# S4 convolution and gated linear attention: three small vectors loaded as rows and turned on TensorE, one table ahead of two copies

## The chip, the core and the metric

The kernel runs on one core of a Trainium2 chip. The metric is the device time of one execution in microseconds (us). A core has five engines that run their own instruction streams in order and wait for each other by semaphores: TensorE (PE; its weight loads are shown apart as PEld), VectorE (DVE), ScalarE (ACT), GpSimd (POOL) and SyncE (SP), which here issues the DMA transfers between HBM and the on-chip memory SBUF. TensorE writes its results to PSUM, from where VectorE or ScalarE copy them out.

## The reference

Two branches work on the same input x = u of [1, 2048, 512] (bfloat16) and are mixed by a gate:

```python
g = sigmoid((x * gate_w).sum(-1, keepdims=True))
a = _A_ref(x, A_re, A_im, B_re, B_im, C_re, C_im, log_dt, Dskip)   # S4: long convolution + skip
b = _B_ref(x, wqkv, w_phi, wo)                                     # linear attention, 32 heads of 16
return g * a + (1 - g) * b
# _A_ref: dt = exp(log_dt); K[d, l] = Re sum_n C exp(dt A l) dt B;  y = irfft(rfft(u) * rfft(K)) + u * Dskip
# _B_ref: phi = [softmax(k w_phi), softmax(-k w_phi)];  o = phi_q (phi_k' v) / (phi_q sum phi_k);  o @ wo
```

Three vectors of 512 numbers matter here: log_dt (the step size of each channel), gate_w (the weights of the gate) and Dskip (the weights of the skip connection).

## The kernel before

The whole kernel is one list of nodes (class `Plan`, L71). A node is a small piece of work on one engine, with what it reads and writes, and, if it needs one, a PSUM tile. The order in which the nodes are emitted, and with it the order on every engine, is written out in a table, `ORDER` (two characters for each node, numbered as they were added). `SIDES` says for each copy out of PSUM (`evict`) whether VectorE or ScalarE makes it; `RINGS` says for each TensorE node that may choose from which ring its PSUM tile comes. There are two such rings in the part that matters, `ps` (digit 0) and `p0` (digit 1), with two buffers each; a third tile in a ring waits until the first one has been read out. Adding a node renumbers those behind it, so the strings differ in many places where the order does not.

What runs in the first 30 us:

- SP issues the loads: sixteen of u in rows (`UD`, L1531, four for each quarter; a node `ud0` to `ud3` is a quarter), the weights `wqk` (L1541, 1 MB) and `WW` (L1544), the six S4 matrices `Are` to `Cim` (L214), and the small vectors. `ldc` (log_dt, L1526), `gw` (gate_w, L1537) and `Dcol_b` (Dskip, L1538) are loaded by column: a tile of 128 partitions with four elements of two bytes in each, number g of partition p being element 128 g + p of the vector. `ld` (L1527) is log_dt once more, broadcast to all partitions.
- VectorE and ScalarE build tables of phases (`tgv`, `tgsv`, `TB`, `TJ`, `TI`) from iota patterns; GpSimd makes the iotas and `Wphi`. `selE` (L456) is one of the tables of VectorE, which takes two small masks (`m`, `b`) and no load.
- TensorE transposes u, eight blocks at a time, into an `xps` tile (L502; eight groups, T8 = 0 to 7, group T8 needs quarter T8 // 2 of u), which is copied to `xT` by VectorE (L149) or ScalarE (L147). T8 = 0 and T8 = 4 come first, before wqk is there, and VectorE copies both. Of the six late groups VectorE copies T8 = 6, ScalarE the rest.
- The columns of wqk are transposed (`wtp`, L528) to `wT`, multiplied by `Wphi` (`wps`, L544), and copied to `WW` and `Wqp`. Of the first two wtp tiles VectorE copies the second one first, and the other after a table instruction.
- The S4 matrices are transposed in pairs (`psri`, L368): pB = (Bre, Bim), pC = (Cre, Cim), pA = (Are, Aim). VectorE multiplies them with the steps (`p_t`, L381) to `ppx`, `pt`, `pmag`, `ppy`. A psri tile is let go when the second product that reads it alone has run: for pB the second of two, for pA the second of two.
- Of the discretised A, pt and ppy are cast and subtracted (L343, L344); SP stores the result to DRAM (`pz`, L348).
- VectorE copies u to `UDp`, and TensorE begins the spectrum of u with it (`psA`, L589), copied to `XAu` by VectorE and ScalarE. Behind this the main part starts: the keys of the attention (`pk`, `Ek`, `Zk`, `vp`), then queries, tables and convolution.

In RINGS, the digits of the eight xps groups are 00000111 and those of pB, pC, pA are 101: T8 = 5, 6 and 7, pB and pA take their tiles from p0, the others from ps.

Of the kernel before, what the change touches and what calls it, by code (L numbers as in the profile page):

```python
# [10 lines left out]
ACT = mybir.ActivationFunctionType  # L11
# [185 lines left out]
def prepare(P, nc, g, evict, psum):  # L197
# [39 lines left out]
    V("ident", lambda: nc.vector.tensor_scalar(out=g.ident[:], in0=g.c128[:], scalar1=g.icol["p"], scalar2=None, op0=ALU.is_equal), r="ic1", w="ic")  # L237

# [255 lines left out]
    E("at3", at3, r="ic wsm mask", w="atm")  # L494
    xt = []
    for T8 in range(8):
        box = Bag()

        def tx(T8=T8, box=box):
            box.ps = psum([128, 4, 4, 4, 32], "xps", BF16)  # L500
            for t in range(8):
                nc.tensor.transpose(out=box.ps[:, t // 4, :, t % 4, :], in_=g.UD[:, 8 * T8 + t, :], identity=g.ident[:])  # L502

        def xe(T8=T8, box=box):
# [1160 lines left out]
```

## Time and profile before

| | |
|---|---|
| median of 3 runs | 254.35 us (252.84 to 256.95) |
| the profiled execution | 252.56 us |
| its span (first to last instruction) | 250.7 us |
| VectorE busy | 233.6 us, 93% |
| ScalarE busy | 222.0 us, 89% |
| TensorE matmuls busy | 201.7 us, 80% |
| DMA | 35.65 MB in 62762 packets, 42112 of them under 512 B |

The profile is of one execution. A group of instructions is printed as start and duration in us, engine, line of the kernel, operation, out<-in with sizes, and how many instructions it joins (x3); the durations of one instruction in its group overlap a little with the next one's, so the time from one start to the next is the pace. In brackets stands the idle time of the engine ahead of the group and what ended it. In the list of idle times a row has the engine, its line, what it waited for, and then the total, how often, and the longest. PE, PEld, DVE, ACT, POOL are the engines, SPq is SP's queue of DMA issues.

### The profile page before, as it was taken

The page shows a single profiled execution, that of the slowest core. Times are in us where ns is not written, and L with a number is a line of the kernel's source. Part 1 is how long each engine was busy: PE and PEld are TensorE (multiplying, and loading weights), DVE is VectorE, ACT ScalarE, POOL GpSimd, SP SyncE. Part 2 cuts the span into 40 slices and gives each one's busy share as a digit, 9 for nine tenths or more (in the row PEclk, how much of TensorE's full clock was granted, in tenths as well). Part 3 has the DMA queues.
Part 4 walks back from the last instruction along what each step waited for, and adds up shares of the span by engine and source line. Part 5 has one row for each costly group of instructions (what it writes and reads, how often), then busy time and mean ns, then how long its engine had stood idle before and what let it go on. Part 6 is the DMA issues. An engine that isn't in the chain of part 4 may idle for free.

```text
span 250.7 us, 9903 instructions
## 1 busy us (share of the span) xinstructions
PE 201.7 (80%) x4411; PEld 141.6 (56%) x4436; DVE 233.6 (93%) x322; ACT 222.0 (89%) x306; POOL 6.3 (2%) x15
## 2 busy tenths in 40 slices
PE   1478899999965468798878778899999789998970
PEld 1377555456743334255556646775667566877550
DVE  6899999989899997999999999999999999999690
ACT  6799899999999989999999999999999999965340
POOL 5400000000000000000000000000000000000000
PEclk9999999999997759999979999999999999999995
DMA  6799200137290487500528138803797878998775
GB/s 167 162 211 164 77 4 3 42 94 191 53 259 0 126 245 224 169 3 4 151 63 235 30 101 222 277 11 86 189 207 191 222 213 212 239 243 151 184 184 82
DMA packets 62762, 35.65 MB, mean 142 GB/s; under 512 B 42112, under 2 KB 58624, under 8 KB 62336
## 3 DMA queue, kind: packets, MB, share of 16 engines
q1 hardware_dynamic: 62720, 35.03, 57.1%
q8 instruction: 34, 0.56, 1.0%
q14 instruction: 8, 0.07, 0.1%
HBM read 21.91 MB, written 13.11 MB: 140 GB/s over the span
## 4 chain that ended last, share of the span: by engine, by line
DVE 40%; PE 19%; ACT 16%; SPq 8%; issue 8%; DMA 7%; DVEq 0%; ACTq 0%
DVE R L1126 5%; DVE t L1302 4%; DVE A L1109 4%; DMA XUX<-XUd 3%; ACT Eq L68 3%; PE vp L755 3%; SPq L1531 3%; DVE A L1114 3%; PE pk L707 3%; DVE R L1130 3%; DVE Zk L734 2%; SPq L214 2%; DVE E L1061 2%; PE psB L614 2%; DVE Eq L912 2%
## 5 line engine op out<-in xcount | busy, mean ns | idle before, releaser
L181 PEld LDWEIGHTS <-A 128*32 128x32 bf16 x1664 | 28.4, 160 | 6.3 <-issue 3.4
L181 PE MATMUL kps<-R,A 128*32 128x64 bf16 x1664 | 30.2, 230 | 1.9 <-DVE A L1114 0.6
L68 ACT ACTIVATE cs<-args 128x1024 bf16<-128x1024 f32 x32 | 30.8, 1049 | 0.4 <-PE args L1025 0.4
L1130 DVE TENSOR_TENSOR R<-E,cs 128x2048 bf16<-128x2048 bf16 x16 | 19.5, 1220 | 0.0
L1109 DVE TENSOR_TENSOR A<-Ctab,Dtab 128x2048 bf16<-128x2048 bf16 x16 | 19.5, 1220 | 0.0
L1126 DVE TENSOR_TENSOR R<-E,cs 128x2048 bf16<-128x2048 bf16 x16 | 19.5, 1220 | 0.0
L1114 DVE TENSOR_TENSOR A<-Ctab,Dtab 128x2048 bf16<-128x2048 bf16 x16 | 19.5, 1220 | 0.0
L147 ACT CAST Zr<-psz 128x1024 bf16<-128x1024 f32 (+1 forms) x17 | 16.5, 975 | 2.7 <-issue 1.2
L147 ACT CAST XK<-psB 128x1024 bf16<-128x1024 f32 (+1 forms) x15 | 15.1, 1012 | 3.9 <-PE psB L194 2.3
L147 ACT CAST XA<-psA 128x1024 bf16<-128x1024 f32 (+1 forms) x16 | 15.6, 1008 | 3.2 <-PE psA L188 3.2
L755 PE MATMUL vp<-WW,xT 128*128 128x512 bf16 x59 | 17.5, 414 | 0.8 <-issue 0.7
L614 PE MATMUL psB<-XAu,TB 64*128 64x128 bf16 x256 | 11.8, 248 | 7.4 <-ACT xst L147 5.2
L1302 DVE TENSOR_TENSOR t<-XUX,XK 128x2048 bf16<-128x2048 bf16 x14 | 17.1, 1220 | 0.3 <-ACT XK L147 0.3
L68 ACT ACTIVATE Ek<-pk 128x512 bf16<-128x512 f32 x32 | 16.8, 603 | 0.4 <-PE pk L707 0.2
L68 ACT ACTIVATE Eq<-pq 128x512 bf16<-128x512 f32 (+1 forms) x28 | 16.8, 715 | 0.2 <-PE pq L841 0.2
L68 ACT ACTIVATE E<-args 128x1024 bf16<-128x1024 f32 x16 | 16.8, 1060 | 0.0
L1328 PE MATMUL psz<-t,TI 128*128 128x512 bf16 x49 | 14.6, 380 | 2.0 <-ACT cs L68 0.5
L841 PE MATMUL pq<-xT,Wqp 128*128 128x512 bf16 x64 | 15.7, 381 | 0.6 <-ACT Eq L68 0.6
L614 PEld LDWEIGHTS <-TB 64*128 64x128 bf16 x256 | 9.5, 109 | 11.3 <-issue 11.1
L707 PE MATMUL pk<-WW,xT 128*128 128x512 bf16 x57 | 15.5, 380 | 0.5 <-issue 0.2
L734 DVE TENSOR_REDUCE Zk<-Ek 128x64 f32<-128x1024 bf16 x12 | 14.0, 1211 | 0.0
L65 ACT ACT_TABLE_LOAD x10 | 12.8, 1283 | 0.2
(215 smaller groups left out, 492.4 us busy)
## 6 DMA issues: line engine op xcount, KB each, us to landing
XUX<-XUd SPq DMA_DIRECT2D x24, 256.0 KB, 4.1
XUd<-xst SPq DMA_DIRECT2D x8, 512.0 KB, 3.1
ax<-apd SPq DMA_DIRECT2D x16, 256.0 KB, 4.7
Zd<-Zr SPq DMA_DIRECT2D x14, 256.0 KB, 4.0
ZT<-Zd SPq DMA_DIRECT2D x12, 256.0 KB, 5.3
UD<-in_A_u_dram SPq DMA_DIRECT2D x16, 128.0 KB, 4.2
XUd<-xst SPq DMA_DIRECT2D x8, 256.0 KB, 4.0
XUX<-XUd SPq DMA_DIRECT2D x4, 512.0 KB, 6.3
```

The lines of the kernel that those rows point to most:

```text
L68: return self.nc.scalar.activation(**kw)
L147: self.nc.scalar.copy(out=o, in_=i)
L181: nc.tensor.matmul(kps[32 * dj:32 * dj + 32, g4, e, :], lhsT=A[:, ka, :, :, d].rearrange("p a b -> p (a b)"), rhs=R[:, kr, d, :], start=(i ...
L614: nc.tensor.matmul(box.ps[:, c2, sl, :], lhsT=fc.TB[rows, b0:b0 + 2].rearrange("p a b -> p (a b)"), rhs=X.t[rows, k, r0 + sl].rearrange("p ...
L707: nc.tensor.matmul(box.ps[:], lhsT=xT[:, st, kt, :], rhs=g.WW[:, kt, :], start=(kt == 0), stop=(kt == 3))
L734: nc.vector.tensor_reduce(out=K.Z[:, u].rearrange("p g h -> p (g h)"), in_=K.E[:, u].rearrange("p g (h f) -> p (g h) f", f=16), axis=mybir ...
L755: nc.tensor.matmul(box.ps[:], lhsT=xT[:, st, kt, :], rhs=g.WW[:, 4 + kt, :], start=(kt == 0), stop=(kt == 3))
L1109: nc.vector.tensor_tensor(out=c.A[:, 0:2].rearrange("p o a b c -> p (o a) b c"), in0=g.C[U // 8][:, 0:2, :, d0 % 256:d0 % 256 + 32].rearra ...
L1114: nc.vector.tensor_tensor(out=c.A[:, 2:4].rearrange("p o a b c -> p (o a) b c"), in0=g.C[U // 8][:, 1:3, :, d0 % 256:d0 % 256 + 32].rearra ...
L1126: nc.vector.tensor_tensor(out=c.R[:, :, :, 32:64], in0=t.E[:, 1].unsqueeze(1).to_broadcast([128, 2, 32, 32]), in1=t.cs[:], op=ALU.mult)
L1130: nc.vector.tensor_tensor(out=c.R[:, :, :, 0:32], in0=t.E[:, 0].unsqueeze(1).to_broadcast([128, 2, 32, 32]), in1=t.cs[:, ::-1, :, ::-1], o ...
L1302: nc.vector.tensor_tensor(out=box.t, in0=Ls[r0 // ns].X[:], in1=box.XK[:].unsqueeze(1).to_broadcast([128, 2, 1024]), op=ALU.mult)
```

## The change

The three loads by column go. In their place SP loads each vector as four rows of 128 contiguous elements: 12 rows of 256 bytes together, into the first 12 partitions of `zrow` (a tile that is not used until the gate is computed much later). TensorE turns these 12 rows with one more transposition, right behind the eight of T8 = 4 and into the same PSUM tile (its third, unused, slot). VectorE copies the 128x12 result to a tile `vecs`, of which ldc, gw and Dcol_b are now slices.

The nodes of xps and xT are added earlier in the list (the order of adding, not of running), and the strings ORDER, SIDES and RINGS are new. The rings of the xps and psri tiles are the same as before. The order differs in these places; names are those of the tiles with a running number, which counts differently in the two programs.

SP, from its first instruction: UD, then wqk and the small loads. Before:

```order
L1531 DMA UD<-in_A_u_dram 32x16x128 x4
L1541 DMA wqk<-in_B_wqkv_dram 128x4x1024
L214 DMA Are<-in_A_A_re_dram 128x4x128
L1536 DMA wc<-in_B_w_phi_dram 128x4x16
L1537 DMA gw<-in_gate_w_dram 128x4x1
L1538 DMA Dcol_b<-in_A_Dskip_dram 128x4x1
L214 DMA Aim<-in_A_A_im_dram 128x4x128
L214 DMA Bre<-in_A_B_re_dram 128x4x128
L1526 DMA ldc<-in_A_log_dt_dram 128x4x1
L1527 DMA ld<-in_A_log_dt_dram 128x512
```

And now:

```order
L1541 DMA UD_105<-in_A_u_dram 32x16x128 x4
L1537 DMA zrow_69<-in_A_log_dt_dram 4x128
L1537 DMA zrow_69<-in_gate_w_dram 4x128
L1537 DMA zrow_69<-in_A_Dskip_dram 4x128
L1549 DMA wqk_113<-in_B_wqkv_dram 128x4x1024
L214 DMA Are_106<-in_A_A_re_dram 128x4x128
L1546 DMA wc_114<-in_B_w_phi_dram 128x4x16
L214 DMA Aim_107<-in_A_A_im_dram 128x4x128
L214 DMA Bre_109<-in_A_B_re_dram 128x4x128
L1533 DMA ld_112<-in_A_log_dt_dram 128x512
```

The three row loads stand ahead of wqk; the three loads by column, which stood behind it, are gone.

VectorE in the late stage, from the product of Aim with the step to the first products of pA (psri_374 before, psri_414 now; pB is psri_317 in both). Before:

```order
L341 TENSOR_TENSOR pt0_163<-Aim_108,dt2_306 128x512
L381 TENSOR_TENSOR ppx_160<-psri_317,pt2_165 128x512
L343 CAST pt1_164<-pt0_163 128x512
L344 TENSOR_TENSOR pt1_164<-pt0_163,pt1_164 128x512
L381 TENSOR_TENSOR ppx_160<-psri_317,pt2_165 128x512
L149 COPY UDp_395<-UD_106 128x16x2x32
L381 TENSOR_TENSOR pt0_163<-psri_374,pt2_165 128x512
```

And now:

```order
L364 TENSOR_TENSOR pt0_161<-Aim_107,dt2_306 128x512
L404 TENSOR_TENSOR ppx_158<-psri_317,pt2_163 128x512
L366 CAST pt1_162<-pt0_161 128x512
L149 COPY xT_68<-xps_398 128x1024
L367 TENSOR_TENSOR pt1_162<-pt0_161,pt1_162 128x512
L404 TENSOR_TENSOR ppx_158<-psri_317,pt2_163 128x512
L149 COPY UDp_426<-UD_105 128x16x2x32
L404 TENSOR_TENSOR pt0_161<-psri_414,pt2_163 128x512
```

The copy of T8 = 6 (xps_398; before it was xps_445, the last instruction ahead of the first XAu cast) now stands between the cast and the subtraction.

ScalarE in the same stage, from the second WW cast. Before:

```order
L147 CAST WW_85<-wps_273 128x1024
L147 CAST Wqp_84<-wps_336 128x1024
L147 COPY xT_68<-xps_348 128x1024
L147 COPY xT_68<-xps_363 128x1024
L147 COPY xT_68<-xps_383 128x1024
L147 CAST Wqp_84<-wps_408 128x1024
L147 COPY xT_68<-xps_422 128x1024
L147 COPY xT_68<-xps_432 128x1024
```

And now:

```order
L147 CAST WW_85<-wps_273 128x1024
L147 CAST Wqp_84<-wps_336 128x1024
L147 COPY xT_68<-xps_348 128x1024
L147 COPY xT_68<-xps_359 128x1024
L147 COPY xT_68<-xps_369 128x1024
L147 COPY xT_68<-xps_379 128x1024
L147 COPY xT_68<-xps_388 128x1024
L147 CAST Wqp_84<-wps_438 128x1024
```

The five copies now follow each other, and the second Wqp cast stands behind them. xps_388, the fifth, is T8 = 7.

On TensorE the transpositions of Are and Aim, those of Cre and Cim, and the second wps of Wqp, which stood between the late xps groups, now stand behind all six of them, in that order; T8 = 6 (xps_398) is the last of the six. Early on VectorE, `selE` stood behind the two copies of T8 = 0 and T8 = 4 and now stands ahead of them, and the copy to `vecs` stands between the two. GpSimd's order is the same.

The diff, with the strings cut to their first lines and what only renames left out:

```diff
-    ORDER = ("0H0I000K0J0M190S0L0s0t0u0U0W0X0B0C0D0T0d0e0f2x0y0z0A2L2v0g0h0i2J2K2M2y2R0102031d2w0N0_0Y0V2T100j0k0l0P1114120405060Z2U16"
...
+    ORDER = ("0K0L00120M141t1a130v0w0x0m0n0o1c1e1f0E0F0G1b0d0e0f2R0B0C0D0Y2P2Q0g0h0i0Z0V0W0X2S2V0102031x151j1g1d2X1k0j0k0l171l1o1m0405"
...
-    SIDES = ("100001110111000000000101000101010111101001011100000000000100101010000001110001001010100000000000000010000000000000000000"
+    SIDES = ("000011101111000000000101000101010111101001011100000000000100101010000001110001001010100000000000000010000000000000000000"
...
-    RINGS = ("101000001110010101100000000000000000000000100000000000000001011100100000001111101101110000100001001110011110100111101101"
+    RINGS = ("000001111010010101100000000000000000000000100000000000000001011100100000001111101101110000100001001110011110100111101101"
...
-    P.dma("ld", 0.8, 2.0, lambda: g.load_ld(), rw=("", "ldc ldb"), move=0.5, cnt=2)
+    P.dma("ld", 0.8, 2.0, lambda: g.load_ld(), rw=("", "ldb"), move=0.5)
+    P.dma("rows", 1.5, 2.0, lambda: g.load_rows(), rw=("", "rows"), move=0.1, cnt=3)
...
-    P.dma("wsm", 1.5, 2.0, lambda: g.load_small(), rw=("", "wsm"), move=0.6, cnt=3)
+    P.dma("wsm", 0.5, 2.0, lambda: g.load_small(), rw=("", "wsm"), move=0.3)
...
+        def tx(T8=T8, box=box):
+            box.ps = psum([128, 4, 4, 4, 32], "xps", BF16)
+            for t in range(8):
+                nc.tensor.transpose(out=box.ps[:, t // 4, :, t % 4, :], in_=g.UD[:, 8 * T8 + t, :], identity=g.ident[:])
+            if T8 == 4:
+                nc.tensor.transpose(out=box.ps[:, 2, 0, 0, 0:12], in_=g.rows, identity=g.ident[0:12, 0:12])
+
+        def cw(box=box):
+            nc.vector.tensor_copy(out=g.vecs[:], in_=box.ps[:, 2, 0, 0, 0:12])
...
+        a = P.add("PE", "xps", tx, take=[("ps", "p0")], rw=(f"ud{T8 // 2} ic" + (" rows" if T8 == 4 else ""), ""))
+        cv = [V("cvec", cw, w="wsv ldc", deps=[a])] if T8 == 4 else []
+        xt.append(evict("xT", xe, [a] + cv))
...
-        g.gw = aq.tile([128, 4], BF16, name="gw")
-        g.Dcol_b = aq.tile([128, 4], BF16, name="Dcol_b")
+        g.vecs = aq.tile([128, 12], BF16, name="vecs")
+        g.ldc, g.gw, g.Dcol_b = g.vecs[:, 0:4], g.vecs[:, 4:8], g.vecs[:, 8:12]
+        g.rows = g.zrow[0:12, 0, 0:64].bitcast(BF16)
...
         def load_ld():
-            with nc.allow_non_contiguous_dma(reason="small"):
-                nc.sync.dma_start(out=g.ldc[:], in_=A_log_dt.rearrange("(g p) -> p g", p=128))
             nc.sync.dma_start(out=g.ld_b[:], in_=A_log_dt.partition_broadcast(128))
+
+        def load_rows():
+            for k, v in enumerate((A_log_dt, gate_w, A_Dskip)):
+                nc.sync.dma_start(out=g.rows[4 * k:4 * k + 4], in_=v.rearrange("(g p) -> g p", p=128))
...
-                nc.sync.dma_start(out=g.gw[:], in_=gate_w.rearrange("(kt p) -> p kt", p=128))
-                nc.sync.dma_start(out=g.Dcol_b[:], in_=A_Dskip.rearrange("(kt p) -> p kt", p=128))
```

More of the change, by code (lines that the diff above doesn't have):

```diff
@@ L237, in prepare, with xe @@
     V("ident", lambda: nc.vector.tensor_scalar(out=g.ident[:], in0=g.c128[:], scalar1=g.icol["p"], scalar2=None, op0=ALU.is_equal), r="ic1", w="ic")
+    xt = []
+    for T8 in range(8):
+        box = Bag()
+        def tx(T8=T8, box=box):
[6 more added lines that the diff above has]
+            nc.vector.tensor_copy(out=g.vecs[:], in_=box.ps[:, 2, 0, 0, 0:12])
+        def xe(T8=T8, box=box):
+            i = box.ps[:, 0:2]
+            box.ps = None
+            return g.xT[:, 2 * T8:2 * T8 + 2].rearrange("p j k s -> p (j k s)"), i.rearrange("p j k c q -> p (j k c q)")
+        a = P.add("PE", "xps", tx, take=[("ps", "p0")], rw=(f"ud{T8 // 2} ic" + (" rows" if T8 == 4 else ""), ""))
+        cv = [V("cvec", cw, w="wsv ldc", deps=[a])] if T8 == 4 else []
+        xt.append(evict("xT", xe, [a] + cv))
     P.add("POOL", "iota", lambda: iota_f(nc, F.col[:], [[16, 32], [1024, 64]], 8), rw=("ic0", "col"))
@@ L327, in dtc @@
         F.dtc = g.up.tile([128, 4], F32, name="dtc")
-        act(out=F.dtc[:], in_=g.ldc[:], func=ACT.Exp)
+        act(out=F.dtc[:], in_=g.ldc, func=ACT.Exp)
     S("dtc", dtc, r="act ldc", w="dtc")
@@ L493, in at3 @@
         nc.gpsimd.memset(at.eps[:], 1e-6)
[L494 to L504, printed above, removed]
-            i = box.ps[:, 0:2]
-            box.ps = None
-            return g.xT[:, 2 * T8:2 * T8 + 2].rearrange("p j k s -> p (j k s)"), i.rearrange("p j k c q -> p (j k c q)")
-        a = P.add("PE", "xps", tx, take=[("ps", "p0")], rw=(f"ud{T8 // 2} ic", ""))
-        xt.append(evict("xT", xe, [a]))
+    E("at3", at3, r="ic wsv mask", w="atm")
     kp = fold(P, nc, g, evict, psum, 512, lambda: g.WW[:, 0:4, :], "wT1")
@@ L677, in gc @@
         nc.vector.reciprocal(out=g.gT[:], in_=G.z[:])
-    a = P.add("PE", "gps", ga, xt, take=["ps"], rw=("wsm", ""))
+    a = P.add("PE", "gps", ga, xt, take=["ps"], rw=("wsv", ""))
     b = P.add("DVE", "g_b", gb, [a], drop=["psum"])
```

45 lines of the change are left out of this document (22 added, 23 removed).

## The prediction

> **What bounds the kernel now.** I read the first part of the profile's page, then the busy time by stretches of the span, then the chain of waits and the idle times of the first 34 us, the only part in which the change moves anything. The page:
>
> ```profile
> span 250.7 us, 9903 instructions
> PE 201.7 (80%) x4411; PEld 141.6 (56%) x4436; DVE 233.6 (93%) x322; ACT 222.0 (89%) x306; POOL 6.3 (2%) x15
> ```
>
> VectorE (DVE) is busy for 93% of the span and ScalarE (ACT) for 89%. A share of the whole span hides where the slack is, so the next view gives stretches (length, then busy time of PE, PEld, DVE, ACT, POOL, the granted clock, DMA share, GB/s):
>
> ```profile
> core 0: us, PE busy (x) PEld busy (x) DVE busy (x) ACT busy (x) POOL busy (x), PEclk, DMA share, GB/s
> 20.00:28.00 8.00, 5.96 (x79) 5.04 (x79) 7.96 (x16) 6.99 (x9) 0.00 (x0) 1.00 0.79 159
> 28.00:60.00 32.00, 31.34 (x546) 17.59 (x553) 31.11 (x43) 30.78 (x59) 0.00 (x0) 1.00 0.21 58
> 100.00:150.00 50.00, 41.35 (x1056) 26.84 (x1055) 49.54 (x58) 49.82 (x74) 0.00 (x0) 0.97 0.34 97
> 150.00:200.00 50.00, 44.44 (x1134) 33.53 (x1138) 49.97 (x54) 48.71 (x58) 0.00 (x0) 1.00 0.69 173
> ```
>
> From 20 to 28 us VectorE idles 0.04 us; from 28 to 60 it idles 0.89 of 32, and later 0.46 and 0.03 of 50. So whatever the first 28 us lose or gain on VectorE goes through to the end almost one to one; there is no slack behind to swallow it. What VectorE did at the edge of that stretch, from the chain of waits (start, us, what):
>
> ```profile
> 5.88 3.09 SPq L214
> ...
> 18.16 3.86 DMA UD<-in_A_u_dram
> 22.02 0.02 issue
> 22.04 0.42 DVE UDp L149
> ```
>
> The chain walks back from the first UDp copy through a load of the input and SP's queue. But the load landed at 22.02 and VectorE, which had been busy without a pause, came to it at 22.04: a tie. Loads that land earlier buy nothing unless VectorE also comes earlier.
>
> **The late stage: the moved copy.** This is the large term. VectorE's and ScalarE's rows of that place in the trace of before:
>
> ```profile
> 20.38 0.42 DVE L343 CAST pt<-pt 128x512 bf16<-128x512 f32 x1
> 20.83 0.69 DVE L344 TENSOR_TENSOR pt<-pt,pt 128x512 bf16<-128x512 f32 x1
> 21.44 0.68 DVE L381 TENSOR_TENSOR ppx<-psri,pt 128x512 f32<-128x512 f32 x1
> 22.04 0.42 DVE L149 COPY UDp<-UD 128x1024 bf16<-128x1024 bf16 x1
> ...
> 26.96 0.68 DVE L149 COPY xT<-xps 128x1024 bf16<-128x1024 bf16 x1
> 27.56 1.22 DVE L149 CAST XAu<-psA 128x1024 bf16<-128x1024 f32 x1
> ```
>
> ```profile
> 20.58 2.85 ACT L147 COPY xT<-xps 128x1024 bf16<-128x1024 bf16 x3
> 23.66 1.01 ACT L147 CAST Wqp<-wps 128x1024 bf16<-128x1024 f32 x1 [0.22 <-PE wps L544]
> 24.57 1.94 ACT L147 COPY xT<-xps 128x1024 bf16<-128x1024 bf16 x2
> ```
>
> ```profile
> 15.73 1.91 PE L528 MATMUL wtp<-ident,wqk 128*128 128x128 bf16 x16
> 19.43 1.33 PE L502 MATMUL xps<-ident,UD 128*128 128x128 bf16 x16
> 20.73 0.38 PE L368 MATMUL psri<-ident,Are 128*128 128x128 bf16 x4
> 20.95 0.39 PE L368 MATMUL psri<-ident,Aim 128*128 128x128 bf16 x4
> 21.65 0.61 PE L502 MATMUL xps<-ident,UD 128*128 128x128 bf16 x8 [0.31 <-ACT xT L147]
> ```
>
> VectorE's only late xT copy stood at 26.96, last before the XAu cast, where its input had been ready for long. The change puts it right behind the cast at 20.38. That copy reads the xps group of T8 = 6, and this group's PSUM tile comes from ring p0, as those of T8 = 5 and 7 and of psri for pB and pA do. p0 has two buffers. One still holds psri of pB (Bre, Bim), because the second product that reads it stands behind the moved copy on VectorE. So the other passes from T8 = 7 to T8 = 6 to psri of pA. TensorE can start T8 = 6 only when T8 = 7 has been copied out, and that is the fifth xT copy of ScalarE, which now stand in one run ahead of the second Wqp cast. VectorE works in order: behind the waiting copy are queued the subtraction of 20.83, pB's second product, all four UDp copies, the products of pA and pC, and XAu. For UDp in turn TensorE's psA waits, then ScalarE's XAu and all Ek work.
>
> The size: three copies took 2.85 us and two 1.94, so one comes 0.91 after the other (difference of the rows) and the last runs about 1.03. Five from 20.58 end at 20.58 + 4 x 0.91 + 1.03 = 25.25. TensorE's eight transpositions take 0.61: 25.86; I allow 0.15 for the two hand-overs (ACT to PE, PE to DVE; no row has them apart): 26.0. VectorE is free at 20.38 + 0.42 = 20.80. It idles 5.2 us. The copy itself is the same work in another place (26.96 to 27.56, 0.60). The rest, 20.83 to 26.96, is 6.13, so XAu starts at 26.0 + 0.60 + 6.13 = 32.7 instead of 27.56: **+5.2**.
>
> The psri of pA, Are and Aim, follow the copy (0.38 and 0.39, overlapping, 0.61 together) and are hidden by the subtraction, the product and the UDp copy, which start 0.61 and 0.60 apart and end with 0.42. The psA matmuls now come straight behind their UDp copies, and the second Wqp cast comes to ScalarE behind its own wait; what stood there at leisure is now in line with VectorE. I take 0.3 for it, between 0 and the 0.8 that ScalarE idled for psA here already (row below). With it: **+5.5**.
>
> ```profile
> 27.82 1.01 ACT L147 CAST XAu<-psA 128x1024 bf16<-128x1024 f32 x1 [0.79 <-PE psA L589]
> 32.30 1.03 PE L755 MATMUL vp<-WW,xT 128*128 128x512 bf16 x4
> ```
>
> SP's store of pz also waits for that subtraction, and the WW load behind it in SP's queue goes out some 5 us later; its reader, vp at 32.30, moves by as much, so nothing is added.
>
> **The start: the row loads.** SP's rows, the idle times, and the rows between:
>
> ```profile
> 2.75 0.49 SPq L1541 DMA_DIRECT2D wqk<-in_B_wqkv_dram  x1
> ...
> 4.38 0.72 SPq L1537 DMA_DIRECT2D gw<-in_gate_w_dram  x1
> 5.15 0.69 SPq L1538 DMA_DIRECT2D Dcol_b<-in_A_Dskip_dram  x1
> ```
>
> ```profile
> DVE xT L149 <- PE xps L502: 1.7, 1, 1.7
> PE wtp L528 <- DMA wqk<-in_B_wqkv_dram: 2.0, 1, 2.0
> ```
>
> ```profile
> 8.48 1.22 DVE L456 TENSOR_TENSOR selE<-m,b 128x1024 bf16<-128x1024 bf16 x1
> 11.88 0.68 DVE L149 COPY wT<-wtp 128x1024 bf16<-128x1024 bf16 x1
> 17.31 0.17 DVE L333 TENSOR_SCALAR dt<-dtc 128x4 f32<-128x4 f32 x1
> ```
>
> ```profile
> 9.20 1.89 PE L528 MATMUL wtp<-ident,wqk 128*128 128x128 bf16 x16 [1.96 <-DMA wqk<-in_B_wqkv_dram]
> ```
>
> ```profile
> GB/s 0 15 224 203 164 340 356 350 66 18 195 72 131 211 242 205 208 213 211 203 191 215 162 148 71 243 240 0 0 0 0 0 0 0 0 0 16 8 0 0
> wqk<-in_B_wqkv_dram SPq DMA_DIRECT2D x1, 1024.0 KB, 6.4
> gw<-in_gate_w_dram SPq DMA_DIRECT2D x1, 1.0 KB, 5.9
> ```
>
> selE (1.22) fills the 1.7 us in which VectorE waited for xps; the new copy to vecs costs between 0.1 and 0.2 (the nearest row is the 128x4 dt, 0.17). The extra weight load and 12-column matmul on TensorE are at most one of the 0.12 us transpositions (1.89 / 16). VectorE would be some 1.4 us (1.7 less 0.17 and a hand-over of 0.1) earlier at its first wT copy, 10.5 instead of 11.88. But that copy needs all 16 wtp transpositions, hence wqk, and wqk is now issued behind three row loads of about 0.54 us each: at 4.38 instead of 2.75. It landed 6.4 after issue, at 9.15. Two bounds: with the same 6.4 it lands at 10.8. In the GB/s row (one number per us) the four early UD loads, issued from 0.74 on, moved first bytes in the second us, some 1.3 us after issue; wqk's three full slots, 5 to 8, came behind them. If wqk was merely queued, it now starts 1.3 behind its issue at 5.7, moves for 3.0 and lands 1.1 later, as it did: 9.8. The wT copy then starts 9.8 + 1.89 + 0.1 = 11.8 (no change) or 12.8 (+0.9). I take 10.2 to 10.3, +0.5, nearer the queued case, since TensorE's wait of 1.96 shows that wqk had only its bytes to wait for. wT starts the chain that leads to ScalarE's xT copies (wps, the wtp of wT2, WW, Wqp), so this comes on top: **+0.5**, between -0.7 (wqk unmoved) and +0.9.
>
> The element-wise loads that go cost SP 0.72 and 0.69, and the load behind them 3.09 (above). [...] In my sum it is worth 0: the loads come earlier, by up to that 3.09, and VectorE doesn't.
>
> **Sum:** 5.5 + 0.5 = +6.0. On the profiled execution, 252.56 (span 250.7 and 1.86 around it), 258.6. The median of the runs shown is 254.35 (252.84 to 256.95), with it 260.4. I put the forecast between: **259.5**. Within 2%, 5.1 us, is about what a measurement of this kernel can't tell from no change.
>
> **The rivals.**
> *The loads decide, and nothing waits (not slower).* If VectorE's moved copy finds T8 = 6 ready at 20.8, which needs a free p0 buffer some 4.5 us before ScalarE's fifth copy ends, the stage keeps its length. Then the start's 1.4 us, or at most SP's 3.09, come through: 249.5 to 251.2. For it speaks the chain, which runs through SP and the UD load; against it the tie at 22.02, and above all the order of the copies. Chance 0.10.
>
> *The wait comes, but smaller.* wqk lands early (-0.7), ScalarE starts its five copies earlier than 20.58, and idle pieces between 60 and 100 us, the least filled stretch, take some of it back:
>
> ```profile
> 60.00:100.00 40.00, 28.52 (x492) 19.23 (x494) 37.19 (x65) 37.97 (x53) 0.00 (x0) 0.83 0.52 145
> ```
>
> VectorE idles 2.8 us there, ScalarE 2.0. If 1 us is given back beside the 0.7 and the 0.5 not spent: +3.5 to +5, 256.5 to 258.5. Chance 0.18.
>
> *The wait comes and TensorE slows down.* At 15.73 us 16 transpositions took 1.91, at 21.65 8 took 0.61: nearly half the pace against full, with the change of pace inside the 16 of 19.43 (1.33). In the changed kernel TensorE idles some 1.9 us ahead of T8 = 6 and 3 to 4 us ahead of psA. If it falls back to half pace, T8 = 6 costs 0.6 more and the first psA and pk matmuls 1 to 1.5: +7 to +8, about 261 to 262. [...] No run here shows a fall back yet. Chance 0.12.
>
> *The rows land late.* The neighbour gw took 5.9 us from issue to landing; so long a time puts the last row load (issued at 3.8) at 9.7, and VectorE's vecs copy, with selE done, waits for it from about 8 on. Under 9 us the wait is hidden by that for wqk; at 9.7 TensorE's early groups and wtp come late too: +6.5 to +7.5. Chance 0.04.
>
> My forecast, +5 to +7, has what is left, 0.56. Slower by over 2%: 0.56 + 0.12 + 0.04, less 0.05 for the part of the forecast near 5.1 us: 0.67. Faster by over 2%, past anything a load is worth here: 0.03. Within 2%: 0.30. The range leaves out the first rival (0.10) and a tail above: 256.0 to 262.8.
>
> **What will show it.** Right, if VectorE idles about 5 us ahead of an xT copy on PE's xps, TensorE waits 1 to 2 us for ScalarE's xT ahead of that group, and XAu starts near 33; if wtp still waits for wqk, which lands at 9.8 or later; if SP's 3.09 us is gone and the UD loads land earlier, without use. Wrong, if that xT copy starts by 22 us, if UDp waits for its load again, or if the shift at 60 us is not the shift at the end.

## The result, and the profile after

The changed kernel takes 261.92 us (median of 6 runs, 260.24 to 265.93) against 254.72 of the kernel before (6 runs, 252.84 to 257.01): 1.0298 times as long, with a 95% interval of 1.0253 to 1.0343. That is some 7.2 to 7.6 us more. The profiled execution of this measurement was a slow one (265.93), so the rows below are those of a second measurement of the same kernel, which gave 1.0294 [1.0248, 1.0339] and whose profiled execution took 261.46.

Its page and its busy time by stretches (us; busy PE, PEld, DVE, ACT, POOL; granted clock, DMA share, GB/s):

```profile
span 259.7 us, 9932 instructions
PE 207.3 (80%) x4437; PEld 143.0 (55%) x4437; DVE 234.5 (90%) x323; ACT 222.1 (86%) x306; POOL 5.6 (2%) x15
```

```profile
20.00:24.00 4.00, 2.04 (x28) 1.58 (x26) 0.67 (x2) 4.00 (x5) 0.00 (x0) 0.97 0.74 107
24.00:28.00 4.00, 2.12 (x19) 1.87 (x18) 1.76 (x3) 1.13 (x2) 0.00 (x0) 0.50 0.01 1
28.00:34.00 6.00, 3.19 (x23) 2.62 (x22) 5.43 (x12) 1.54 (x2) 0.00 (x0) 0.50 0.42 111
```

VectorE does the same work (234.5 us against 233.6) in a longer span. From 20 to 28 us, where it was busy for 7.96 of 8, it now works 2.43. And the clock that TensorE is granted reads 0.50 from 24 to 34 us; in the profile of before it read 1.00 in all of these stretches.

VectorE, ScalarE and TensorE in the late stage of the changed kernel:

```profile
20.25 0.42 DVE L366 CAST pt<-pt 128x512 bf16<-128x512 f32 x1
26.23 0.69 DVE L149 COPY xT<-xps 128x1024 bf16<-128x1024 bf16 x1 [5.56 <-PE xps L247]
...
33.62 1.23 DVE L149 CAST XAu<-psA 128x1024 bf16<-128x1024 f32 x1 [0.57 <-PE psA L597]
...
38.17 1.23 DVE L149 CAST XAu<-psA 128x1024 bf16<-128x1024 f32 x1 [1.71 <-PE psA L597]
```

```profile
20.34 4.80 ACT L147 COPY xT<-xps 128x1024 bf16<-128x1024 bf16 x5
```

```profile
21.44 0.61 PE L247 MATMUL xps<-ident,UD 128*128 128x128 bf16 x8 [1.23 <-DMA UD<-in_A_u_dram]
22.36 0.61 PE L247 MATMUL xps<-ident,UD 128*128 128x128 bf16 x8 [0.31 <-ACT xT L147]
23.38 0.70 PE L247 MATMUL xps<-ident,UD 128*128 128x128 bf16 x8 [0.42 <-DMA UD<-in_A_u_dram]
25.18 1.01 PE L247 MATMUL xps<-ident,UD 128*128 128x128 bf16 x8 [1.10 <-ACT xT L147]
...
32.51 1.93 PE L597 MATMUL psA<-W,UDp 128*128 128x256 bf16 x8 [2.81 <-DVE UDp L149]
34.23 3.46 PE L715 MATMUL pk<-WW,xT 128*128 128x512 bf16 x8
```

And of the kernel before, the rows of psA and pk on TensorE and the second XAu on VectorE:

```profile
26.51 1.19 PE L589 MATMUL psA<-W,UDp 128*128 128x256 bf16 x8 [1.10 <-ACT xT L147]
27.54 1.89 PE L707 MATMUL pk<-WW,xT 128*128 128x512 bf16 x7
```

```profile
30.31 1.22 DVE L149 CAST XAu<-psA 128x1024 bf16<-128x1024 f32 x1
```

Read from below: VectorE's moved copy waits 5.56 us for T8 = 6 (25.18), which TensorE begins 1.10 us after it could, when ScalarE's fifth copy is done (20.34 + 4.80 = 25.14). The first XAu comes 6.06 us later than before (33.62 against 27.56), the second 7.86 (38.17 against 30.31): between the two another 1.8 us are lost, where TensorE does psA in 1.93 instead of 1.19 and eight pk in 3.46, where seven took 1.89.

Behind that nothing is gained or lost for most of the span. One of the late VectorE rows, first of before and then of the changed kernel:

```profile
180.11 1.22 DVE L1302 TENSOR_TENSOR t<-XUX,XK 128x2048 bf16<-128x2048 bf16 x1
```

```profile
188.38 1.22 DVE L1310 TENSOR_TENSOR t<-XUX,XK 128x2048 bf16<-128x2048 bf16 x1
```

That is 8.27 us behind, 150 us after the place where the time was lost. Near the end VectorE loses some more: it waits 1.20 us for psy where it waited 0.52, and 2.33 for bps where it waited 1.24, and the spans differ by 9.0 (259.7 against 250.7). What causes this was not tried. The traces show more than the 7.2 to 7.6 us of the times partly because the profiled execution of before, 252.56, lies below its median.

The start, with SP's loads, the first wT copies on VectorE and what GpSimd does beside them:

```profile
2.76 0.43 SPq L1537 DMA_DIRECT2D zrow<-in_A_log_dt_dram  x1
3.23 0.25 SPq L1537 DMA_DIRECT2D zrow<-in_gate_w_dram  x1
...
3.86 0.41 SPq L1549 DMA_DIRECT2D wqk<-in_B_wqkv_dram  x1
...
6.85 2.09 SPq L1533 DMA_DIRECT2D ld<-in_A_log_dt_dram  x1
```

```profile
9.69 0.81 DVE L290 TENSOR_SCALAR tgv<-tgc,one 128x1024 int32<-128x1024 f32 x1 [0.15 <-ACT TB L68]
11.13 0.69 DVE L149 COPY wT<-wtp 128x1024 bf16<-128x1024 bf16 x1 [0.62 <-PE wtp L536]
11.73 1.55 DVE L290 TENSOR_SCALAR tgv<-tgc,one 128x1024 int32<-128x1024 f32 x1
13.21 0.67 DVE L149 COPY wT<-wtp 128x1024 bf16<-128x1024 bf16 x1
```

```profile
9.20 1.89 PE L536 MATMUL wtp<-ident,wqk 128*128 128x128 bf16 x16 [1.20 <-DMA wqk<-in_B_wqkv_dram]
```

```profile
11.79 0.95 POOL L791 MEMSET KVbd<- 128x1024 bf16 x1
```

The second of these wT copies in the kernel before:

```profile
13.33 0.67 DVE L149 COPY wT<-wtp 128x1024 bf16<-128x1024 bf16 x1
```

wqk is issued 1.1 us later than before, and still wtp begins at 9.20, as before. VectorE reaches its first wT copy 0.75 us early, and is 0.12 early at the second (13.21 against 13.33), where the table instruction between them takes 1.55 us, 0.92 before; GpSimd clears KVbd beside it.

### The profile page after: what moved, and what is told of

Its sections match the earlier page's. It is cut to its first block, busy times and chain, and to the rows that moved or that the text cites. A ratio compares the mean times of both kernels' runs of the same rounds, so it can differ in the third digit from the quotient of the medians.

```text
span 264.1 us, 9932 instructions
## 1 busy us (share of the span) xinstructions
PE 208.5 (79%) x4437; PEld 144.5 (55%) x4437; DVE 234.8 (89%) x323; ACT 222.4 (84%) x306; POOL 5.5 (2%) x15
## 4 chain that ended last, share of the span: by engine, by line
PE 27%; ACT 25%; DVE 23%; DMA 9%; SPq 7%; issue 7%; DVEq 0%; ACTq 0%
PE pk L715 5%; ACT cs L68 5%; ACT Eq L68 4%; SPq L1541 4%; PE vp L763 3%; ACT E L68 3%; PE psB L622 2%; DMA ZT<-Zd 2%; DVE t L1310 2%; PE kps L181 2%; DMA XUd<-xst 2%; ACT XA L147 2%; PE psy L830 2%; ACT L65 2%; DVE vr L772 2%
## 5 line engine op out<-in xcount | busy, mean ns | idle before, releaser
L715 PE MATMUL pk<-WW,xT 128*128 128x512 bf16 x64 | 17.7, 412 | 0.0
L1336 PE MATMUL psz<-t,TI 128*128 128x512 bf16 x60 | 15.2, 379 | 1.8 <-ACT cs L68 0.5
L597 PE MATMUL psA<-W,UDp 128*128 128x256 bf16 x64 | 10.4, 299 | 5.1 <-DVE UDp L149 2.8
## 6 DMA issues: line engine op xcount, KB each, us to landing
XUX<-XUd SPq DMA_DIRECT2D x24, 256.0 KB, 4.3
ax<-apd SPq DMA_DIRECT2D x16, 256.0 KB, 4.8
Zd<-Zr SPq DMA_DIRECT2D x14, 256.0 KB, 3.3
ZT<-Zd SPq DMA_DIRECT2D x12, 256.0 KB, 5.3
XUd<-xst SPq DMA_DIRECT2D x8, 256.0 KB, 5.0
```

Source lines behind the costliest of these rows:

```text
L715: nc.tensor.matmul(box.ps[:], lhsT=xT[:, st, kt, :], rhs=g.WW[:, kt, :], start=(kt == 0), stop=(kt == 3))
```

## The experiments

My theory was that the order of the late stage alone costs the time, by the chain fifth ScalarE copy, p0 buffer, T8 = 6, VectorE. Against it stood the row loads (wqk delayed, or u earlier), and TensorE's pace as a part of its own. All ratios are to the kernel before on the same chip.

### The late order alone

The kernel before, with this order of the late stage on the engines and nothing else changed:

```diff
 VectorE: CAST pt
+         COPY xT (T8 = 6)
          TENSOR_TENSOR pt, ppx, ... UDp ...
-         COPY xT (T8 = 6)
          CAST XAu
 ScalarE: COPY xT x3
-         CAST Wqp
          COPY xT x2
+         CAST Wqp
 TensorE: psri pA, pC and wps behind all six xps groups
```

> The kernel before with nothing but the changed order of the late stage (the five ScalarE copies in a run, VectorE's copy of T8 = 6 behind the cast, the psri of pA and pC and the second wps behind all six groups); the loads by column stay. If the late order alone costs the time: 1.025 to 1.032 of the kernel before (+6.5 to +8 us), VectorE idle 5 to 6 us ahead of that copy, XAu at 33 to 34. If the row loads carry part of it, because the last quarter of u then comes at 23.8 instead of 22.0: at least 1 us less, 1.015 to 1.022.

1.0394 [1.0347, 1.0442], above the 1.025 to 1.032 expected. Once more, beside the experiment after the next:

> The first experiment once more beside the one above, for a second trace of its loads: 1.035 to 1.044 of the kernel before. If its late landing of the last quarter was an accident of one execution, the trace now shows a wait of T8 = 7 for it of under 1 us and a ratio near the changed kernel's 1.029.

1.0231 [1.0153, 1.0309]. VectorE and TensorE in the first and the second of these:

```profile
26.06 0.77 PE L502 MATMUL xps<-ident,UD 128*128 128x128 bf16 x8 [2.33 <-DMA UD<-in_A_u_dram]
...
28.98 0.69 DVE L149 COPY xT<-xps 128x1024 bf16<-128x1024 bf16 x1 [7.54 <-PE xps L502]
```

```profile
24.64 0.61 PE L502 MATMUL xps<-ident,UD 128*128 128x128 bf16 x8 [0.89 <-DMA UD<-in_A_u_dram]
...
27.40 0.69 DVE L149 COPY xT<-xps 128x1024 bf16<-128x1024 bf16 x1 [5.93 <-PE xps L502]
```

The late order by itself costs about as much as the whole change: 1.0294 lies between the two. The two measurements of one kernel, taken on two chips, don't agree within their intervals, by 1.6% or some 4 us. Of this the traces show 2.5 at the second XAu (40.85 and 38.33). 1.6 of it comes from one load: T8 = 7 waited 2.33 us for the last quarter of u in the one and 0.89 in the other, and VectorE 7.54 and 5.93. The rest is TensorE's pace, seven pk in 2.97 and in 2.04. In both, VectorE also came to the wait 0.64 to 0.67 us later than in the trace of before (the cast ahead of it at 21.02 and 21.05 against 20.38), which the late order doesn't explain. In the old order a wait of T8 = 7 for this load can be hidden (0.78 us in the run of row loads below, where XAu comes no later); under the late order it is on the path.

To see whether this load explains it, the same kernel with that quarter issued ahead of Cre and Cim:

```diff
 SP: UD x8
+    UD x4
     Cre, Cim
-    UD x4
```

> The kernel before with the changed order of the late stage (as in the first experiment, loads by column kept) and the last quarter of u loaded ahead of Cre and Cim. The first experiment took 1.039 where the changed kernel takes 1.029; its last quarter landed at 25.9 instead of 23.3 to 23.8, and T8 = 7 waited 2.3 us for it. If that landing is what the loads by column cost under the late order: T8 = 7 starts at about 24.5 or sooner, VectorE idles about 6 instead of 7.5 us, and the ratio is 1.028 to 1.034. If the difference lies elsewhere: 1.036 to 1.042.

1.0295 [1.0206, 1.0384]: inside what was expected, but the interval also holds 1.0231, the late order without the move on the same chip. T8 = 7 started at 24.65, VectorE idled 5.73 us. Whether loads by column make the landing later can't be told from these: the change's own 1.029 lies between the two measurements without row loads.

### The rest alone: row loads and selE

For this the changed kernel gets the late order of before. That order is not allowed in it as it stands. `x_tmp`, the node that opens the pool of UDp, waits for every node that was added ahead of it, and the change adds xps and xT earlier: so all eight xT copies had to be written down before the first UDp copy. I took them out of that list:

```diff
-    sx = P.add("X", "x_tmp", shift, [n for n in P.nodes if n.eng != "SP" and n.eng not in ("D", "W")])
+    sx = P.add("X", "x_tmp", shift, [n for n in P.nodes if n.eng != "SP" and n.eng not in ("D", "W") and n.name not in ("xps", "xT", "cvec")])
...
-    ORDER = (the late stage as changed)
+    ORDER = (the late stage as before)
```

> The changed kernel (row loads ahead of wqk, vecs, selE early) with the late stage in the order of before; for that the node that opens the pool of UDp no longer waits for the xT copies. If the late order alone costs the time: 0.995 to 1.004 of the kernel before, no idle time of VectorE between 13 and 27 us, wT at about 11.2, XAu at 27 to 28. If the row loads cost by delaying wqk: 1.004 to 1.010. If, freed of the late order, the loads decide: 0.988 to 0.994.

> The second experiment once more beside the one above: 0.996 to 1.004 of the kernel before, second wT copy at 13.3.

1.0001 [0.9965, 1.0037] and, the second time, 0.9964 [0.9929, 0.9999]. VectorE in the first of them:

```profile
13.33 0.67 DVE L149 COPY wT<-wtp 128x1024 bf16<-128x1024 bf16 x1
...
27.56 1.22 DVE L149 CAST XAu<-psA 128x1024 bf16<-128x1024 f32 x1
```

XAu at 27.56, to the hundredth as before. So the row loads, the extra transposition, vecs and the early selE are worth nothing, or at most a few tenths of a per cent; the change's time is all in the order. The row loads took SP less time than those by column (0.25 to 0.43 us each against 0.51 to 0.72 in the kernel before), and nobody waited for it.

The tgv of 1.55 us beside GpSimd's clearing looks like what ate VectorE's lead. So, in this kernel, the clearing was moved ahead of Wphi:

```diff
     def at1(e):
+        at.KVbd = g.aq.tile([128, 8, 128], BF16, name="KVbd")
+        nc.gpsimd.memset(at.KVbd[:], 0.0)
...
     def f1():
-        at.KVbd = g.aq.tile([128, 8, 128], BF16, name="KVbd")
-        nc.gpsimd.memset(at.KVbd[:], 0.0)
```

> The second experiment (row loads, late stage in the order of before) with one move more: GpSimd's clearing of KVbd stands ahead of Wphi instead of behind it, so that it runs in VectorE's slack near 4 us instead of beside the table instruction at 11.9. That instruction took 1.55 us beside it and 0.81 for its like a little earlier, and so ate the 0.6 us that VectorE was ahead. If so: it takes 0.8 to 0.9, the second wT copy starts at about 12.7 instead of 13.3, and 0.5 to 0.6 us come through: 0.996 to 0.999 of the kernel before, hardly to be told from 1 by the time, but from the trace. If something else holds the place: the second wT copy stays at 13.3 and the ratio at 1.000.

0.9991 [0.9961, 1.0020], and the second wT copy came at 13.56, no earlier. VectorE and GpSimd in it:

```profile
3.83 2.13 DVE L290 TENSOR_SCALAR tgv<-tgc,if,one 128x1024 int32<-128x1024 f32 x2
...
10.29 2.03 DVE L290 TENSOR_SCALAR tgv<-tgc,one 128x1024 int32<-128x1024 f32 x1 [0.83 <-ACT TB L68]
```

```profile
3.74 0.95 POOL L494 MEMSET KVbd<- 128x1024 bf16 x1
10.33 1.05 POOL L496 TENSOR_TENSOR Wphi<-wc,mask 128x512 bf16<-128x512 bf16 x1 [5.64 <-DMA wc<-in_B_w_phi_dram]
```

A miss. The clearing now slowed the two tgv at 3.83 (2.13 instead of 1.53), ScalarE's tables came later, and the tgv that waits for them ran beside Wphi instead, 2.03 us against 0.81. The place of the meeting moved, and its price stayed.

### Only the moved copy put back

The changed kernel, with T8 = 6 alone put back to the end; ScalarE's run of five and the psri behind T8 = 7 stay. The list of `x_tmp` is shortened as above, since this copy too stands behind UDp copies:

```diff
 VectorE: CAST pt
-         COPY xT (T8 = 6)
          TENSOR_TENSOR pt, ppx, ... UDp ...
+         COPY xT (T8 = 6)
          CAST XAu
 TensorE: xps (T8 = 7)
-         xps (T8 = 6)
          psri pA, pC, wps
+         xps (T8 = 6)
```

> The changed kernel with only T8 = 6 (its transpositions and VectorE's copy) put back to the end of the late stage; the run of five ScalarE copies and the psri behind T8 = 7 stay. If the place of VectorE's copy is the cause: VectorE doesn't wait at that copy, and only at the first product of pA, whose transpositions now stand behind T8 = 7 on TensorE (its part of u comes at up to 23.8, 0.6 for T8 = 7, 0.4 for Are: 24.9 against 22.4 on VectorE): +2 to +3 us, 1.008 to 1.013. If the run of five copies and the moved psri cost as much by themselves: 1.02 or more.

1.0197 [1.0131, 1.0263]: less came back than expected (1.008 to 1.013). VectorE and TensorE:

```profile
25.46 0.69 DVE L404 TENSOR_TENSOR pt<-psri,pt 128x512 f32<-128x512 f32 x1 [3.05 <-PE psri L391]
```

```profile
23.61 0.96 PE L247 MATMUL xps<-ident,UD 128*128 128x128 bf16 x8 [0.56 <-DMA UD<-in_A_u_dram]
```

The wait at the copy is gone, and as expected VectorE waits for pA instead, 3.05 us (2.5 expected: TensorE is already at half pace, 0.96 for eight transpositions). XAu came at 30.66, 3.1 later than before, the second at 34.74, 4.4 later: the slow TensorE again (psA in 1.45 us and six pk in 2.57; before, 1.19 and seven in 1.89). So putting the moved copy back returns half of the loss at the first XAu (3.0 of 6.06) and a third of the time (1.0 of 2.9%), no more: the psri behind the last quarter of u cost 3 us by themselves as soon as the copy's wait is not there. The two waits don't add; the longer one hides the other.

### The PSUM ring of T8 = 6, and the load ahead of it

One digit of RINGS, the seventh, which is that of T8 = 6 (the first ten are shown):

```diff
-    RINGS = ("0000011110..."
+    RINGS = ("0000010110..."
```

> The changed kernel with one digit of RINGS changed: the PSUM tile of T8 = 6 comes from ring ps, whose buffer is free from ScalarE's third copy on. If the shared p0 buffer (T8 = 6 waits for the fifth copy) is the last wait in the chain: T8 = 6 follows T8 = 7 on TensorE at once, VectorE's copy starts 0.7 us behind T8 = 7, at 25.2 instead of 26.7, and its idle time is about 4.5 instead of 6.0: 1.5 us back, 1.022 to 1.025. The rest of the idle time is the wait of T8 = 7 for the last quarter of u (23.8), which the forecast left out. If the buffer is not the cause: no change, 1.028 to 1.033.

1.0216 [1.0186, 1.0247].

```profile
24.86 0.69 DVE L149 COPY xT<-xps 128x1024 bf16<-128x1024 bf16 x1 [4.18 <-PE xps L247]
```

```profile
23.77 1.05 PE L247 MATMUL xps<-ident,UD 128*128 128x128 bf16 x16 [0.79 <-DMA UD<-in_A_u_dram]
```

T8 = 6 follows T8 = 7 at once (16 in a row, 1.05 us), TensorE keeps its pace until psA (each half of a psri in 0.38 to 0.39 us, the granted clock at 1.00 from 20 to 28; psA then took 1.60), and VectorE waits 4.18 instead of 5.56 us. So the shared buffer was the last link of the chain, and 1.4 us of it; in this run the link before is the last quarter of u.

The changed kernel with that quarter issued ahead of Cre and Cim (the edit on SP as above):

> The changed kernel with the last quarter of u loaded ahead of Cre and Cim instead of behind them (256 KB less ahead of it, at 170 to 200 GB/s 1.3 to 1.5 us). If the chain runs through that load: T8 = 7 starts as soon as TensorE is free (23.0 instead of 23.9), but ScalarE's fifth copy then only follows its fourth (24.1 instead of 24.6), so 0.4 to 0.5 us come back at VectorE's copy, 0.002 below the changed kernel's ratio, hardly clear of noise in the time but plain in the trace. If ScalarE's run of copies alone sets the fifth's end: no change at that copy.

1.0271 [1.0232, 1.0311], not told from 1.0294 by the time.

```profile
20.40 4.73 ACT L147 COPY xT<-xps 128x1024 bf16<-128x1024 bf16 x5
```

```profile
25.82 0.69 DVE L149 COPY xT<-xps 128x1024 bf16<-128x1024 bf16 x1 [5.08 <-PE xps L247]
```

```profile
22.42 1.05 PE L247 MATMUL xps<-ident,UD 128*128 128x128 bf16 x16 [0.31 <-ACT xT L147]
25.17 0.61 PE L247 MATMUL xps<-ident,UD 128*128 128x128 bf16 x8 [1.70 <-ACT xT L147]
...
32.10 1.92 PE L597 MATMUL psA<-W,UDp 128*128 128x256 bf16 x8 [3.73 <-DVE UDp L149]
```

With the load out of the way the chain is the one of the forecast: five copies without a pause, T8 = 6 in 0.61, idle time 5.08. The fifth copy ends at 25.13, as in the changed kernel (25.14), so the load had cost nothing there; the 0.4 us are those of T8 = 6 (0.61 against 1.01). The second XAu came at 36.73, 1.44 earlier than in the changed kernel; of this the times show 0.6 us, within their noise.

### TensorE kept busy

The changed kernel with extra work in TensorE's waits, first in all of them:

```diff
             if T8 == 4:
                 nc.tensor.transpose(out=box.ps[:, 2, 0, 0, 0:12], in_=g.rows, identity=g.ident[0:12, 0:12])
+            for t in range({3: 16, 1: 4, 0: 12, 7: 14, 6: 8}.get(T8, 0)):
+                nc.tensor.transpose(out=box.ps[:, 2 + t // 4 % 2, :, t % 4, :], in_=g.UD[:, 8 * T8 + t % 8, :], identity=g.ident[:])
...
                 box.ps = psum([128, 4, 256], "psA")
+                for i in range(10 if h == 0 and g4 == 0 else 0):
+                    nc.tensor.matmul(box.ps[:, 0:2, :].rearrange("p a b -> p (a b)"), lhsT=g.ident[:], rhs=fc.TB[:, 1:9].rearrange("p a b -> p (a b)"),
+                                     start=True, stop=True, skip_group_check=True)
```

> The changed kernel with extra work on TensorE that fills its waits of the late stage: 4 to 16 more transpositions into the unused half of the xps tiles of T8 = 3, 1, 0, 7, 6, and 10 matmuls of 512 columns into the first psA tile ahead of its own. No result changes. If the slow pace of TensorE behind its waits costs part of the time (in the changed kernel's trace T8 = 6 took 1.01, psA 1.93 and the first eight pk 3.62 us): these take 0.6, 1.2 and 2, and 1.5 to 2.5 us come back, 1.019 to 1.024. If the slow pace is hidden or is due to something else: 1.028 to 1.033, or more where the extra work itself is in the way.

1.0474 [1.0415, 1.0534]: it became slower. The copies had to wait for the extra transpositions into their tiles:

```profile
26.25 1.01 ACT L147 COPY xT<-xps 128x1024 bf16<-128x1024 bf16 x1 [1.58 <-PE xps L251]
```

VectorE's copy went to 29.22, behind its 8.55 us of idle time. But behind it the eight pk took 1.89 us, and the second XAu came at 38.96, 9.74 after that copy, where the changed kernel has 11.94 (38.17 less 26.23). T8 = 6 itself still took 1.01 us: the extra transpositions, with TensorE busy for 3.21 of the 4 us from 20 to 24, did not hold its pace. In its trace the kernel falls another 6 us behind between 120 and 210 us; what caused that was not tried. So only the matmuls ahead of psA were kept:

> The changed kernel with extra work only in TensorE's wait for UDp: 10 matmuls of 512 columns into the first psA tile ahead of its own; nothing extra in the xps groups, so no copy is held up by it. If TensorE's slow pace behind that wait costs time, the first eight pk take 1.9 instead of 3.6 us, the second XAu no longer waits 2.2 us, and 2 to 2.7 us come back: 1.019 to 1.023. If not: 1.028 to 1.033.

1.0242 [1.0203, 1.0280], with these rows:

```profile
30.06 4.00 PE L596 MATMUL psA<-TB,ident 128*128 128x512 bf16 x10
33.89 1.04 PE L600 MATMUL psA<-W,UDp 128*128 128x256 bf16 x8
34.77 1.89 PE L718 MATMUL pk<-WW,xT 128*128 128x512 bf16 x8
```

```profile
37.28 1.22 DVE L149 CAST XAu<-psA 128x1024 bf16<-128x1024 f32 x1
```

VectorE's wait at the second XAu (1.71) is gone, though the extra matmuls are themselves in the way at the first (4.00 us). The copy of T8 = 6 stood at 26.80, 0.57 later than in the changed kernel, and the second XAu is 0.89 earlier: 1.5 us came back, where 2 to 2.7 were expected. In the time it is 0.5%, 1.3 us, with intervals that overlap a little; the trace shows it plainly. So TensorE's fall to half pace (psA in 1.93 and eight pk in 3.46 us in the changed kernel, 1.04 and 1.89 here) is a part of the change's cost of its own, by the trace; the time alone would not show it.

No version that was run is clearly faster than the kernel before.

## Why the prediction was right, and where it was not

**The mechanism was right.** Slower by over 2% was forecast, at 259.5 us in a range of 256.0 to 262.8; 261.92 was measured. The late term was found as it stands: five ScalarE copies in a run (4.80, forecast 4.67), T8 = 6 behind the fifth, VectorE idle 5.2 (5.56; 5.08 where the load is out of the way), +5.2 to +5.5 at the first XAu (+6.06), and no slack behind: at 188 us the kernel is 8.3 behind. The experiments show the links: without the late order nothing is lost, with the late order alone all of it, with another ring VectorE waits 1.4 us less. The hand-overs in the sum (0.15 for the two around T8 = 6, 0.1 for one at the start) were my estimate, taken from no row; with the last quarter first the two were 0.04 each (25.13 to 25.17, 25.78 to 25.82), and the one at the start 0.04 in the changed kernel (11.09 to 11.13). What the forecast didn't say is that without the moved copy VectorE would still wait 3.05 us, for pA. And its sign that the shift at 60 us is the shift at the end held only roughly: 8.02 (Zk, 53.14 before and 61.16 now) against 9.0.

**The term that was mis-sized is TensorE's pace.** It was a rival with a chance of 0.12 and a price of +1 to +2 over the forecast, and it came: the granted clock at 0.50 from 24 to 34 us, T8 = 6 in 1.01 instead of 0.61, 1.8 us more between the first and the second XAu, 1.3 to 1.5 of it back with TensorE kept busy. The idle time of 5.56 (0.4 of it the slow T8 = 6), the 0.57 ahead of the first XAu and these 1.8 make the 7.9 of the trace; the forecast had 5.2 and 0.3, and 0.5 for wqk. The error was in the chance: the rival named the waits itself (1.9 ahead of T8 = 6, 3 to 4 ahead of psA). In the run with the last quarter first they came nearly so: behind 1.70 us T8 = 6 kept its pace (0.61), behind 3.73 us psA did not (1.92). So the larger part of the rival's price hung on a wait that the forecast itself expected. And "No run here shows a fall back yet" overlooked a row on the page of before, the granted clock in tenths, in 40 slices of 6.27 us:

```profile
PEclk9999999999997759999979999999999999999995
```

The 13th to 15th slices (75 to 94 us) read 7, 7 and 5; there 16 psB matmuls took 0.62 us at 83.33, behind a wait of 1.48, and 1.04 at 85.19, behind one of 1.24. In the changed kernel T8 = 7 took 0.70 at 23.38 and T8 = 6 1.01 at 25.18, with no pause over 1.23 us ahead of them in the rows above. What brought this fall about is not shown; the pace held in a run with similar pauses:

```profile
20.00:24.00 4.00, 1.94 (x30) 1.58 (x27) 0.74 (x2) 4.00 (x5) 0.00 (x0) 1.00 0.88 126
24.00:28.00 4.00, 1.90 (x29) 1.65 (x29) 2.18 (x5) 1.12 (x2) 0.00 (x0) 1.00 0.01 1
```

These are the stretches of the run with the last quarter first. TensorE is busy for 1.94 and 1.90 of 4 us, no more than in the changed kernel (2.04 and 2.12), and the granted clock stays at 1.00.

**wqk was wrong.** The step that took "nearer the queued case" and still +0.5 failed: row loads took SP 0.25 to 0.43 each, not 0.54, and wqk was issued 1.1 us later, yet wtp, which waits for it, began at the same 9.20. What happened is the low end of the text, -0.7 for a wqk that doesn't move: VectorE was 0.75 us early at wT. But this too was given back, beside GpSimd (the table instruction of 1.55 us, 0.92 before), which the forecast didn't have. The term measured 0.

**The loads.** "The loads come earlier, and VectorE doesn't" is half wrong. SP's long wait didn't go; it moved from Aim (3.09) to ld (2.09). And T8 = 7 still waits for the last quarter of u, because the change needs it earlier than the kernel before did. The sum had ScalarE's fifth copy follow the fourth without asking what T8 = 7 reads. A row of the trace of before would have told:

```profile
24.35 1.05 PE L502 MATMUL xps<-ident,UD 128*128 128x128 bf16 x16 [0.26 <-DMA UD<-in_A_u_dram]
```

In the execution shown the wait was 0.42 us and cost nothing; in the first measurement of the late order alone it was 2.33, and VectorE idled 1.6 us longer than in the second.

**Rivals.** The first (loads decide) needed T8 = 6 ready at 20.8; it was at 26.2. The late rows didn't come: vecs waited 0.28 us, for TensorE. The smaller wait didn't come either, since nothing between 60 and 190 us gave anything back.

**What was told wrong ahead of the prediction.** The early pair of xps groups is T8 = 4 and 5, both of quarter 2, not T8 = 0 and 4; the late six are 2, 3, 1, 0, 7 and 6. No step rests on it. The title names the loads and the table; the time went with the order of the late stage. And that order is no free choice of the table: the list of what `x_tmp` waits for demands it.

## What to carry to other kernels

Ask of an instruction that moves up on a full engine what it waits for, link by link (PSUM buffer, the copy that frees it, the load that feeds it), and then what stands behind it: an early load is worth nothing where nobody waits, and a late one costs nothing until the order puts it on the path. Putting one instruction back shows what comes back, not what it cost, if another wait stands behind it. Where a new wait leaves TensorE idle, look at the pace of its next matmuls: here, with the last quarter first, psA took 1.92 us behind a wait of 3.73 (1.19 in the kernel before), and T8 = 6 no more than 0.61 behind one of 1.70. And where a plan collects "everything added so far" as a dependency, moving a definition changes the schedule.

## What the runs showed of the hardware that was not expected

- **VectorE beside GpSimd.** One table instruction (128x1024, f32 to int32) takes 0.80 to 0.81 us with little or nothing beside it, 1.55 beside a memset of 0.95, and 2.03 beside a tensor_tensor of 1.05. In the kernel before, GpSimd paid: the same memset took 1.55 us there, and the table instructions beside it 0.80 and 0.92. Moving GpSimd's work only chose another victim (two table instructions in 2.13 us instead of 1.53, and a third in 2.03). The time added was 0.74 us beside the memset of 0.95 and 1.22 beside the tensor_tensor of 1.05 with three memsets of 0.21 to 0.64 behind it; what brings it about no run here shows.
- **The pace of TensorE** fell in the changed kernel with pauses of 1.23, 0.31, 0.42 and 1.10 us (T8 = 6 in 1.01), and kept up through 1.23, 0.31 and 1.70 with the last quarter first (0.61). T8 = 6 took 1.01 with TensorE busy for 3.21 of the 4 us from 20 to 24 (kept busy), and 0.61 with 1.94. Neither the longest pause nor the busy share of these 4 us tells the runs apart; what does was left open.
- **One kernel, two measurements** of 1.0394 and 1.0231, with intervals that don't meet. The traces show the wait for one load as 2.33 and 0.89 us, and seven pk as 2.97 and 2.04; whether the chip or the occasion makes the difference was not tried.
